# One written order for the first sixteen attention tiles in a fused attention and expert kernel

## The chip, the cores and the metric

The kernel runs on one core of a Trainium2 chip. The metric is the device time of one execution in microseconds (us); less is better. TensorE (PE) does the matmuls and transposes, VectorE (DVE) the elementwise arithmetic, ScalarE (ACT) the transcendental functions and most copies out of the accumulators, GpSimd (POOL) the indirect transfers, and SyncE (SP) issues nearly all plain transfers.

## The reference

Two stages follow one another. The first is a recurrent attention: for each of 4 batches and 8 heads, a 48 by 48 complex state is decayed at every one of 768 steps by a complex factor per row, takes in the outer product of k and v, and is read by q.

```python
mag = np.sqrt(a_re * a_re + a_im * a_im)
scale = np.minimum(mag, 0.999) / (mag + 1e-06)
for t in range(S):
    new_re = ar * S_re - ai * S_im
    new_im = ar * S_im + ai * S_re
    S_re, S_im = (new_re + kv, new_im)
    y[:, :, t] = np.einsum('bhd,bhde->bhe', q[:, :, t], S_re)
```

The second is a mixture of experts on the 3072 rows of 384 that come out: noisy gate logits, the two best of eight experts with softmax weights, and for each expert `relu(x @ w1) @ w2`, with w1 of 384 by 1024.

## The kernel before

Attention is chunked. A tile n is 128 time steps of one batch with all heads; n runs from 0 to 23, four tiles (the four batches) make a group g, and two tiles make a pair m. Inside a chunk the recurrence becomes matmuls; between chunks a state Z per batch is carried.

The change and the prediction name the instructions by an engine letter (A for ScalarE, D for VectorE, P for TensorE), a step and, behind the point, the pair or tile:

- For a pair (`p1`, `p2a`, `p2carry`, `p2s`): A1 is Ln of the real part, A2 its Exp, D1 and D2 the tangent and its square, A3 a Ln, D3 the doubled log magnitude, A4 an Exp, D4 the clipped log decay; A5 is the Arctan, D5 adds the angle carried from the group before, D8 takes absolute values, A7 and A8 are cosine and sine.
- For a tile: P1 sums the angles along time by a triangular matrix, A6 or D6 and D7 take whole turns off (`p2t`); P2 sums the log decays, A9 and A10 are their two Exps, D9 scales q and k by them (`p3`); D10 and D11 multiply q and k by cosine and sine (`p3q`); P3 and P4 transpose q and k, A11 and A12 copy the transposes out (`tr_unit`, line 299); P5a and P5b are the scores, D12a and D12b mask them (`sc_unit`, line 308); P6 is the new part of the state (`st_unit`), D13 adds it to Z (`st_upd`), D15 scales Z (`st_scale`); P7a and P7b make y, A13 copies it out (`y_unit`, line 357); P8 transposes it, A14 copies it (`x_unit`, line 365).
- For a group: G0 is the gate logits (`gate_logits`) and G10 the softmax, the slots and the indirect scatters of rows to the experts' lists (`gate_dispatch`). Their instructions have no names of their own.

All activations go through `phase` (lines 199 and 200), which also orders the loads of the activation table: A1 to A4, A9 and A10 use the table with logarithm and Exp, A5, A7 and A8 the trigonometric one. So there are two table loads in each group, and all A5, A7, A8 of a group stand between them.

Buffers couple the engines: two sets of the three pair tiles `t0`, two `tf`, three `ee`, eight `qk`, six `v`, one PSUM tile `ptr` for the transposes, two `psc` for the scores, two `cum` for P1, P2, P8 and the gates, one `pG` and one `pY`.

Nothing in the program text says which instruction an engine takes next. Each call is entered by `at(step, ...)` at a step number on a time line in which tile n stands at n; the calls are emitted in the order of their steps, and the framework's scheduler then orders every engine's queue by emission order, by priority (`x_unit`, `gate_logits` and `gate_dispatch` have raised ones) and by what its own model of time holds ready. Examples:

```python
at(f - q1 + j * P["d1"], p1, m)
at(n + .5 - P["q"] + i * P["qd"] if n > 1 else f - q3, p3q, n, i)
at(n + P["sc"] + P["sh"] * half, sc_unit, n, half)
at(f - P["lqk"] if g else -14, load_qk, n)
```

The loads stand on SP's one queue. The scatters on POOL wait for the y of a later tile (`PACE`). Behind step 16.5 the expert stage begins to fill in: weights of expert 0 are loaded and split (`load_w1`, lines 501, 502 and 510), its rows are read back and transposed (`x_T`), and its first matmuls (`mm1`, line 564) are put between the last attention tiles. From about 262 us on only expert work is left, with TensorE nearly always at work.

Of the kernel before, what the change touches and what calls it, by code (L numbers as in the profile page):

```python
# [77 lines left out]
def kernel(  # L78
# [21 lines left out]
    NQ = 2  # L100
# [121 lines left out]
    def p1(m):  # L222

        T0[m] = [pf.tile([128, 2, HD], F32, name=f"t0{i}", bufs=2) for i in range(3)]
        ta, tb, th = (flat(x) for x in T0[m])
        ph = 2 * (2 * m // B)
        re, im = flat(RE[m]), flat(IM[m])
        phase(ph, ta, re, AF.Ln)
        i = 2 * m
        phase(ph, tb, ta, AF.Exp, scale=-1.0, accum_out=bad[:, 0, i:i + 1])  # L230
        nc.vector.tensor_mul(th, im, tb)
        nc.vector.tensor_tensor_reduce(tb, th, th, 1.0, 0.0, OP.mult, OP.max, bad[:, 1, i:i + 1])
        phase(ph, tb, tb, AF.Ln, bias=1.0)
        nc.vector.scalar_tensor_tensor(ta, ta, 2.0, tb, op0=OP.mult, op1=OP.add)
        phase(ph, tb, ta, AF.Exp, scale=-0.5, bias=b_eps)
        nc.vector.scalar_tensor_tensor(ta, ta, 2.0 * math.log(0.999), tb, op0=OP.min, op1=OP.subtract)

    def p2a(m):
        th = flat(T0[m][2])
        phase(2 * (2 * m // B) + 1, th, th, AF.Arctan)  # L240

    def p2carry(m):
        if m >= B // 2:
            th = T0[m][2][0:1]
            b = 2 * m % B
            nc.vector.scalar_tensor_tensor(th, car[:, b:b + 2], -2.0 * math.pi, th, op0=OP.mult, op1=OP.add)

    def p2t(n):
        b, g = bt(n)
        pt = psC.tile([128, 512], F32, name="cum")  # L250
        nc.tensor.matmul(pt[:, :HD], tri_t, T0[n // 2][2][:, b % 2, :], start=True, stop=True)
        if n % 2 == 0:
            TF[n // 2] = pf.tile([128, 2, 2, HD], F32, name="tf", bufs=2)
        tf = TF[n // 2][:, :, n % 2, :]
        if g:
            nc.scalar.activation(tf[:, 1, :], pt[:, :HD], AF.Identity, bias=b_rnd)
            nc.vector.scalar_tensor_tensor(tf[:, 0, :], tf[:, 1, :], -RND, pt[:, :HD], op0=OP.add, op1=OP.subtract)
        else:
            nc.vector.tensor_scalar(tf[:, 1, :], pt[:, :HD], RND, -RND, op0=OP.add, op1=OP.add)
            nc.vector.tensor_sub(tf[:, 0, :], tf[:, 1, :], pt[:, :HD])  # L260
        if g + 1 < NG:
            nc.sync.dma_start(car[:, b, :], tf[127:128, 0, :])

    def p2s(m):

        f, a = (flat(TF[m][:, i]) for i in range(2))
        nc.vector.tensor_scalar(a.bitcast(I32), f.bitcast(I32), 0x7FFFFFFF, None, op0=OP.bitwise_and)
        TR[m] = pq.tile([128, 2, 2, HD], F32, name="tr", bufs=4)
        phase(2 * (2 * m // B) + 1, flat(TR[m][:, 0]), a, AF.Sin, scale=-TWO_PI, bias=b_cos)
        phase(2 * (2 * m // B) + 1, flat(TR[m][:, 1]), f, AF.Sin, scale=-TWO_PI)  # L270

    def p3(n):
        b, g = bt(n)
        pt = psC.tile([128, 512], F32, name="cum")
        nc.tensor.matmul(pt[:, :HD], tri_l, T0[n // 2][0][:, b % 2, :], start=True, stop=True)
        EE[n] = pf.tile([128, 2, HD], F32, name="ee", bufs=3)
        ph = 2 * g + 2 if n > 1 else 0
        phase(ph, EE[n][:, 0, :], pt[:, :HD], AF.Exp)
        phase(ph, EE[n][:, 1, :], pt[:, :HD], AF.Exp, scale=-1.0)
        nc.vector.tensor_mul(QK[n], QK[n], EE[n])  # L280
        ec = ecol[g % 3]
        nc.sync.dma_start(es[n:n + 1, :], EE[n][127:128, 0, :])
        for r in range(2):
            nc.sync.dma_start(ec[64 * r:64 * r + D, b, :], es[n].rearrange("(h d) -> d h", h=H))
# [24 lines left out]

    def st_unit(n):  # L310
        b, g = bt(n)
        if g + 1 == NG:
            return
        x = kh[n % NQ]
        for h in range(H):
            for r in range(2):
                nc.tensor.matmul(pG[64 * r:64 * r + D, h, :], x[:, h, r, 0:D], V[n][:, h, :], start=True, stop=True)

    def st_upd(n):
# [5 lines left out]
        if g:  # L325
            nc.vector.tensor_add(Z[b], Z[b], pG)
        else:
            Z[b] = pa.tile([112, H, D], F32, name=f"z{b}")
            nc.vector.tensor_copy(Z[b], pG)

    def st_scale(n):
# [6 lines left out]
        nc.vector.tensor_mul(Z[b], Z[b], FC[g][:, b, :, None].to_broadcast([112, H, D]))  # L338

    def y_unit(n):  # L340
# [292 lines left out]
    pri = {gdis: P["hg"], x_unit: P["hx"], glog: P["hl"]}  # L633
    for g in range(NG):
        f = B * g + .5
        q1, q2, q3 = P.get(f"s{g}", (P["p1"], P["p2"], P["p3"]))
        for j in range(B // 2):
# [3 lines left out]
            at(f - q2, p2a, m)  # L641
            at(f - q2, p2carry, m)
            at(f - q2 + .01, p2s, m)
        for j in range(B):
            n = B * g + j
            at(f - P["lqk"] if g else -14, load_qk, n)
            at(f - q2 + j * P["dt"], p2t, n)
            at(f - q3 + j * P["d3"] if n > 1 else f - q2 - .25, p3, n)
            for i in range(2):
                at(n + .5 - P["q"] + i * P["qd"] if n > 1 else f - q3, p3q, n, i)  # L650
    for n in range(NT):
        at(n + .5 - P["lv"], load_v, n)
        for i in range(2):
            at(n - P["tr"] + P["tk"] * i, tr_unit, n, i)
        for half in range(2):
            at(n + P["sc"] + P["sh"] * half, sc_unit, n, half)
        at(n + P["st"], st_unit, n)
        at(n + P["y"], y_unit, n)
        at(n + P["up"], st_upd, n)
# [295 lines left out]
```

## Time and profile before

| | us |
|---|---|
| median of 3 runs | 716.5 (715.35 to 717.31) |
| the profiled execution's own time | 712.03 |
| its span, first to last instruction | 710.3 |
| TensorE busy in the span | 663.7 (93%) |
| VectorE busy | 411.6 (58%) |
| ScalarE busy | 327.2 (46%) |
| GpSimd busy | 164.4 (23%) |

The profiled execution is 4.5 us shorter than the median of the timed ones, and 1.7 us longer than its span. Busy shares are means over two unlike stages, attention up to about 262 us and experts behind it. TensorE's records overlap, since its matmuls are pipelined and their ends are modelled.

### The profile page before, as it was taken

What the parts mean: (1) busy time and instruction counts of PE and PEld (TensorE: products, weight loads), DVE (VectorE), ACT (ScalarE), POOL (GpSimd) and SP (SyncE); (2) the same over time, 40 slices, a digit from 0 to 9 for tenths busy, and PEclk for the clock granted to TensorE, in tenths of its full rate; (3) what the DMA queues carried; (4) which work ended last, traced back from release to release, by engine and by line L of the source; (5) the groups of instructions that cost most, each with busy time, mean ns of one, the idle gap of its engine ahead of it and who ended that gap; (6) DMA issues with size and microseconds to landing.
All of it is one profiled execution on the core that took longest, in us unless ns stands there. A gap on an engine that the chain in (4) does not pass through costs nothing. (4 is left out here: it accounts for less than half of the span.)

```text
span 710.3 us, 13286 instructions
## 1 busy us (share of the span) xinstructions
PE 663.7 (93%) x5120; PEld 592.7 (83%) x5120; DVE 411.6 (58%) x907; ACT 327.2 (46%) x541; POOL 164.4 (23%) x183
## 2 busy tenths in 40 slices
PE   1579999999999999999999999999999999999995
PEld 0367687878888979898998998998999899899995
DVE  6788899999998757545237325425524624524311
ACT  5679989897955551324115215215313413413300
POOL 2000001323323225112323122222321411412311
PEclk9879999999999999999999999999999999999998
DMA  7477876653466517225228125325415515502201
GB/s 266 118 228 193 278 204 219 211 194 83 142 167 234 198 67 265 93 77 187 64 82 261 32 82 189 116 85 172 133 42 179 172 42 172 173 23 69 65 33 36
DMA packets 63902, 100.24 MB, mean 141 GB/s; under 512 B 26264, under 2 KB 45989, under 8 KB 63824
## 3 DMA queue, kind: packets, MB, share of 16 engines
q1 hardware_dynamic: 54464, 71.68, 32.7%
q0 software_dynamic: 9360, 27.54, 11.1%
q8 instruction: 46, 0.75, 0.4%
q14 instruction: 32, 0.26, 0.1%
HBM read 68.55 MB, written 31.69 MB: 141 GB/s over the span
## 5 line engine op out<-in xcount | busy, mean ns | idle before, releaser
L613 PE MATMUL po<-w2h,h 128*128 128x384 f32 x768 | 204.2, 339 | 2.1 <-DVE ao L624 2.1
L564 PE MATMUL ph<-x,w1h 128*128 128x512 f32 (+2 forms) x720 | 187.3, 349 | 1.3 <-DVE h L570 0.8
L613 PEld LDWEIGHTS po<-w2h,h 128*128 128x128 f32 x768 | 139.4, 188 | 3.7 <-DVE ao L624 3.6
L564 PEld LDWEIGHTS ph<-x,w1h 128*128 128x128 f32 x720 | 125.7, 189 | 18.8 <-DVE h L570 2.1
L613 PE MATMUL po<-w2l,h 128*128 128x384 f32 x384 | 128.6, 335 | 0.0
L564 PE MATMUL ph<-x,w1l 128*128 128x512 f32 (+2 forms) x360 | 124.6, 347 | 0.0
L625 POOL DMA_INDIRECT out_dram<-ao,ox x52 | 50.9, 979 | 268.0 <-DVE ao L624 238.3
L570 DVE SCALAR_TENSOR_TENSOR h<-ph,h 128x512 fp32r<-128x512 f32 (+2 forms) x144 | 70.0, 506 | 68.5 <-ACT h L566 68.4
L566 ACT ACTIVATE h<-ph 128x512 fp32r<-128x512 f32 (+2 forms) x120 | 60.0, 507 | 102.6 <-PE ph L564 85.4
L624 DVE SCALAR_TENSOR_TENSOR ao<-po,gw,ao 128x384 f32<-128x384 f32 (+1 forms) x52 | 31.8, 613 | 125.1 <-PE po L613 124.8
L421 POOL DMA_INDIRECT xs<-xr,sl x48 | 52.8, 1101 | 207.1 <-ACT t L200 104.3
L545 ACT CAST x<-px 128x512 fp32r<-128x512 f32 (+1 forms) x42 | 21.4, 518 | 125.6 <-PE px L540 125.5
L564 PEld LDWEIGHTS ph<-x,w1l 128*128 128x128 f32 x360 | 68.1, 189 | 7.9
L613 PEld LDWEIGHTS po<-w2l,h 128*128 128x128 f32 x384 | 72.3, 188 | 0.1
L589 POOL DMA_INDIRECT ao<-out_dram,ox x49 | 54.4, 1111 | 51.9 <-DMA out_dram<-ao,ox 32.2
L307 PE MATMUL psc<-qT,kT 112*128 112x128 f32 x384 | 52.1, 281 | 0.0
L307 PEld LDWEIGHTS psc<-qT,kT 112*128 112x128 f32 x384 | 48.1, 196 | 2.5 <-issue 1.1
L356 PE MATMUL pY<-am,v 128*48 128x128 f32 x384 | 41.3, 275 | 1.5 <-DVE am L308 1.5
L501 ACT CAST w2h<-raw 128x768 fp32r<-128x768 f32 x32 | 26.4, 836 | 32.5 <-PE po L613 17.3
L502 DVE TENSOR_TENSOR w2l<-raw,w2h 128x768 fp32r<-128x768 f32 x32 | 30.5, 958 | 14.3 <-ACT w2h L501 13.3
L298 PE MATMUL ptr<-ident,qh 128*112 128x128 f32 x192 | 30.2, 289 | 8.6 <-ACT kT L299 7.9
L308 DVE TENSOR_TENSOR am<-psc,mask 128x512 f32<-128x512 f32 x48 | 32.6, 686 | 7.8 <-PE psc L307 7.7
(210 smaller groups left out, 947.9 us busy)
## 6 DMA issues: line engine op xcount, KB each, us to landing
raw<-in_moe_w_dram SPq DMA_DIRECT2D x24, 512.0 KB, 6.7
raw<-in_moe_w_dram SPq DMA_DIRECT2D x32, 384.0 KB, 3.7
qk<-in_qk_dram SPq DMA_DIRECT2D x24, 384.0 KB, 4.1
xgb<-xs SPq DMA_DIRECT2D x8, 800.0 KB
re<-in_a_dram SPq DMA_DIRECT2D x12, 384.0 KB, 3.3
im<-in_a_dram SPq DMA_DIRECT2D x12, 384.0 KB, 7.1
v<-in_v_dram SPq DMA_DIRECT2D x24, 192.0 KB, 2.5
out_dram<-zero SPq DMA_DIRECT2D x12, 384.0 KB, 5.1
```

The lines of the kernel that those rows point to most:

```text
L307: nc.tensor.matmul(p[:, j, :], KT[n][:, h, :], QT[n][:, h, :], start=True, stop=True)
L308: LAST['am'] = nc.vector.tensor_mul(AM[n][:, 4 * half:4 * half + 4, :], p, mask[:, None, :].to_broadcast([128, 4, 128]))
L356: nc.tensor.matmul(o, V[n][:, h, :], AM[n][:, h, :], start=not g, stop=True, skip_group_check=True)
L421: d = nc.gpsimd.indirect_dma_start(out=xs, out_offset=bass.IndirectOffsetOnAxis(ap=sl[:, kk, b:b + 1], axis=0), in_=XR[g][:, lo + b, :], i ...
L502: d = nc.vector.tensor_tensor(lo, raw_t, hi.bitcast(F32), op=OP.subtract)
L564: LAST['m'] = nc.tensor.matmul(p[:, :c], W1[e, kk][i][:, f * 128:(f + 1) * 128], XW[w, kk][:, j, 0:c], start=(m == 0), stop=(m == len(ms) ...
L566: nc.scalar.activation(h[:, 0:c], p[:, :c], AF.Relu)
L570: LAST['h'] = nc.vector.scalar_tensor_tensor(h[:, dst:dst + b - a], p[:, a:b], 0.0, h[:, a:b].bitcast(F32), op0=OP.max, op1=OP.subtract)
L589: nc.gpsimd.indirect_dma_start(out=ao[j][0:w, :], out_offset=None, in_=out, in_offset=bass.IndirectOffsetOnAxis(ap=OX[e][0:w, j:j + 1], ax ...
L613: LAST['po'] = nc.tensor.matmul(p[:, :DM], HT[w, f][i][:, o:o + 128], W2[f // 2][k2][:, f % 2, :], start=(m == 0), stop=(m == len(ms) - 1))
L624: nc.vector.scalar_tensor_tensor(a, p[0:n, :DM], g, a, op0=OP.mult, op1=OP.add)
L625: nc.gpsimd.indirect_dma_start(out=out, out_offset=bass.IndirectOffsetOnAxis(ap=OX[e][0:n, j:j + 1], axis=0), in_=a, in_offset=None, bound ...
```

## The change

The same instructions are issued; none is added, none goes. A string `ORDER` lists 581 keys: 574 named steps (200 of ScalarE, 204 of VectorE, 170 of TensorE) and the places of seven calls for the gates. It holds tiles 0 to 15 whole but for D13.15, A14.15 and D15.12 and later, of tiles 16 to 19 the steps up to D9 and some behind it, and of pairs 10 and 11 the first steps. Three things are done with it. Each call is emitted at the place of its first key, `-16 + .03 * i`. Loads are emitted early (the first two groups' inputs, six `v` tiles and all constants ahead of everything) or right behind the step that frees their buffer. And on each of ScalarE, VectorE and TensorE every key's first instruction is made to follow the last one of the key before it in the list, without a semaphore: it fixes the order in the queue. Instructions of the gates can still fall between. Tiles behind the list keep their steps. Also, `tf` is now allocated by whichever tile of a pair comes first.

```diff
+    ORDER = """
+        A1.0 A2.0 D1.0 D2.0 A3.0 A1.1 D3.0 A2.1 A4.0 D1.1 D4.0 D2.1 P2.0 A3.1 P2.1 A9.0 D3.1 A10.0 D9.0 A4.1
+        A9.1 D4.1 A10.1 A5.0 D9.1 A5.1 P1.0 P1.1 D6.0 D7.0 P1.2 D6.1 D7.1 D8.0 P1.3 A8.0 D6.2 A7.0 D7.2 D6.3
+        P2.2 D10.0 D7.3 P3.0 D11.0 A8.1 P2.3 D8.1 A11.0 D11.1 P6.0 A7.1 D10.1 P4.0 A1.2 D13.0 P6.1 D13.1 A9.2
+        A2.2 A1.3 D1.2 A10.2 D2.2 A2.3 D9.2 A12.0 D1.3 A3.2 P3.1 A9.3 D2.3 P5a.0 A11.1 D3.2 P5b.0 A3.3 D12a.0
+        A4.2 P4.1 D12b.0 A10.3 D3.3 P7a.0 A12.1 P7b.0 D4.2 A4.3 P5a.1 D9.3 A13.0 P5b.1 D12a.1 A5.2 D10.2 P8.0
+        P7a.1 D11.3 P3.2 A14.0 D5.2 A5.3 D12b.1 A11.2 P1.4 D4.3 P7b.1 A6.4 D5.3 P1.5 A13.1 D7.4 A6.5 D10.3 P1.6
+        D7.5 A6.6 D11.2 P1.7 A8.2 D8.2 P6.2 A6.7 D7.6 A7.2 D7.7 P4.2 D13.2 A8.3 P2.4 D8.3 A12.2 P6.3 A7.3 P5a.2
+        D13.3 A9.4 P2.5 D12a.2 P5b.2 A1.4 P7a.2 D12b.2 A10.4 P3.3 A2.4 D9.4 P7b.2 A9.5 D1.4 A11.3 P2.6 D10.4
...
+        A6.11 P5a.6 A7.4 D7.11 D8.5 P6.5 A8.5 D12a.6 A7.5 P2.8 D11.7 P5b.6 P7b.5 D12b.6 A9.8 A10.8 P2.9 D13.5
+        A13.5 D9.8 P8.4 A1.6 P7a.6 A14.4 A2.6 P6.6 A9.9 P7b.6 D10.8 A10.9 G10.0 A13.6 P3.7 D11.8 P8.6 A11.7
...
+        D7.15 P2.12 D13.8 A8.7 D8.7 P7a.9 D12b.9 A7.7 P6.9 P8.8 D11.11 P7b.9 A14.8 A9.12 P4.10 D13.9 A13.9 P6.10
+        A10.12 A12.10 P8.9 P2.13 A14.9 D9.12 G10.1 A1.8 P5a.10 A9.13 P3.11 A2.8 D11.12 P2.14 A10.13 D12a.10
...
+        D11.13 A7.8 P1.19 D13.12 P4.13 D7.18 A6.19 D11.14 P2.16 A12.13 D7.19 P6.13 D15.11 A8.9 D8.9 P5a.13
+        D11.15 A7.9 P3.14 D12a.13 P5b.13 P7a.13 D12b.13 A11.14 P2.17 A9.16 A10.16 P7b.13 A9.17 A1.10 P4.14
+        A10.17 A13.13 D13.13 P2.18 D9.16 A12.14 G10.2 P6.14 A9.18 A2.10 P3.15 D9.17 A10.18 P5a.14 A11.15 D10.17
...
+        D12b.15 A3.11 P8.14 D3.10 P7b.15 A14.14 D3.11 A4.10 P4.16 D9.19 A13.15 P6.15 A4.11 D4.10 G0.3 A12.16
+        D11.17 P8.15 A5.10
+    """.split()
+    def key(name, ins):
+        K.setdefault(name, []).append(ins)
+        return ins
...
-        phase(ph, ta, re, AF.Ln)
+        key(f"A1.{m}", phase(ph, ta, re, AF.Ln))
...
+    PLACE = {k: -16 + .03 * i for i, k in enumerate(ORDER)}
+    def pos(step, *names):
+        ks = [PLACE[k] for k in names if k in PLACE]
+        return min(ks) if ks else step
+    def behind_key(step, name):
+        return PLACE[name] + .01 if name in PLACE else step
...
-            at(f - P["la"] if g else -20, load_a, m)
-            at(f - q1 + j * P["d1"], p1, m)
+            at(-20 + g if early else behind_key(f - P["la"], f"D1.{m - 2}"), load_a, m)
+            at(pos(f - q1 + j * P["d1"], f"A1.{m}"), p1, m)
...
-            at(f - P["lqk"] if g else -14, load_qk, n)
+            at(-19.5 + g if early else behind_key(f - P["lqk"], f"D11.{n - 8}"), load_qk, n)
...
-        at(n + .5 - P["lv"], load_v, n)
+        at(-18.7 + .01 * n if n < 6 else behind_key(n + .5 - P["lv"], f"P7b.{n - 6}"), load_v, n)
...
-    at(-3, consts2)
+    at(-17, consts2)
     for i in range(N // 256):
-        at(P["co"] + .5 + i, clear_out, i)
+        at(behind_key(P["co"] + .5 + i, f"P8.{i + 3}"), clear_out, i)
...
+    for e in "ADP":
+        ks = [k for k in ORDER if k[0] == e]
+        for a, b in zip(ks, ks[1:]):
+            tc.add_manual_dep(K[b][0].ins, K[a][-1].ins.name, after, reason="order at the start")
```

## Rows read from the trace of the kernel before

**Rows 1.** Busy time by stretch between the A5 steps: us, then each engine's.
```profile
core 0: us, PE busy (x) PEld busy (x) DVE busy (x) ACT busy (x) POOL busy (x), PEclk, DMA share, GB/s
5.72:18.54 12.82, 2.90 (x4) 1.18 (x4) 9.24 (x12) 8.15 (x12) 0.10 (x1) 1.00 0.75 287
18.54:44.23 25.69, 16.93 (x164) 12.26 (x164) 21.67 (x33) 18.58 (x25) 0.00 (x0) 0.80 0.64 174
44.23:74.93 30.70, 27.22 (x255) 21.51 (x256) 25.20 (x39) 28.04 (x43) 0.00 (x0) 0.94 0.67 203
74.93:109.18 34.25, 33.13 (x390) 26.33 (x390) 31.54 (x77) 30.14 (x50) 0.00 (x0) 1.00 0.74 231
109.18:144.78 35.60, 35.03 (x465) 29.91 (x461) 34.34 (x81) 31.22 (x50) 9.77 (x8) 1.00 0.71 218
144.78:181.40 36.62, 35.71 (x467) 29.89 (x464) 34.50 (x82) 30.88 (x50) 12.59 (x14) 1.00 0.47 146
```

**Rows 2.** The same view where attention's end and expert work mix.
```profile
220.00:240.00 20.00, 20.00 (x184) 17.47 (x183) 16.53 (x71) 11.20 (x24) 5.03 (x5) 1.00 0.40 133
```

**Rows 3.** VectorE's waits from 58.1 to 181.4 us: total, times, longest.
```profile
DVE qk L280 <- ACT ee L200: 3.3, 3, 2.1
DVE am L308 <- PE psc L307: 2.6, 4, 1.0
DVE tf L257 <- ACT tf L256: 0.8, 3, 0.4
DVE kh L288 <- PE pG L317: 0.5, 1, 0.5
```

**Rows 4.** Timeline of ScalarE: start, us, line, tiles, [idle before <-releaser].
```profile
7.64 0.84 ACT L200 ACTIVATE t<-re 128x768 f32<-128x768 f32 x1 [1.95 <-DMA re<-in_a_dram]
...
17.25 1.28 ACT L199 ACT_TABLE_LOAD   x1
18.54 1.57 ACT L200 ACTIVATE t<-t 128x768 f32<-128x768 f32 x2
...
31.35 1.64 ACT L200 ACTIVATE ee<-cum 128x384 f32<-128x384 f32 x4
...
35.97 1.04 ACT L299 ACTIVATE kT<-ptr 112x1024 f32<-112x1024 f32 x1
...
44.23 1.58 ACT L200 ACTIVATE t<-t 128x768 f32<-128x768 f32 x2
...
57.17 1.64 ACT L200 ACTIVATE ee<-cum 128x384 f32<-128x384 f32 x4
```

**Rows 5.** Timeline of VectorE, same columns.
```profile
6.72 0.96 DVE L232 CUSTOM_DVE_ANT_0 t<-t 128x768 f32<-128x768 f32 x1
...
25.36 0.96 DVE L288 TENSOR_TENSOR qh<-qk,tr 128x768 f32<-128x768 f32 x1
...
58.08 1.83 DVE L280 TENSOR_TENSOR qk<-qk,ee 128x768 f32<-128x768 f32 x2 [2.14 <-ACT ee L200]
...
63.30 1.28 DVE L308 TENSOR_TENSOR am<-psc,mask 128x512 f32<-128x512 f32 x2
...
65.36 0.55 DVE L329 COPY z<-pG 112x384 f32<-112x384 f32 x1
```

**Rows 6.** Timeline of TensorE: P2 of tiles 0 and 1, transposes of q twice.
```profile
13.42 2.90 PE L275 MATMUL cum<-t,tri_l 128*128 128x384 f32 x4 [13.42 <-DVE t L236]
...
37.06 1.96 PE L298 MATMUL ptr<-ident,qh 128*112 128x128 f32 x8 [5.75 <-ACT kT L299]
...
67.66 1.08 PE L298 MATMUL ptr<-ident,qh 128*112 128x128 f32 x8 [0.45 <-ACT kT L299]
```

**Rows 7.** Busy time and granted clock around the first of those transposes.
```profile
34.00:37.00 3.00, 0.00 (x0) 0.00 (x0) 3.00 (x5) 3.00 (x6) 0.00 (x0) 0.50 0.75 128
```

**Rows 8.** Timeline of SP's issues: a constant, and `qk` of group 1.
```profile
26.02 0.43 SPq L676 DMA_DIRECT2D xs<-none  x1
...
37.97 2.45 SPq L213 DMA_DIRECT2D qk<-in_qk_dram  x4
```

More of the change, by code (lines that the diff above doesn't have):

```diff
@@ L227, in p1 @@
         re, im = flat(RE[m]), flat(IM[m])
-        phase(ph, ta, re, AF.Ln)
+        key(f"A1.{m}", phase(ph, ta, re, AF.Ln))
         i = 2 * m
[L230 to L236, printed above, removed]
+        key(f"A2.{m}", phase(ph, tb, ta, AF.Exp, scale=-1.0, accum_out=bad[:, 0, i:i + 1]))
+        key(f"D1.{m}", nc.vector.tensor_mul(th, im, tb))
+        key(f"D2.{m}", nc.vector.tensor_tensor_reduce(tb, th, th, 1.0, 0.0, OP.mult, OP.max, bad[:, 1, i:i + 1]))
+        key(f"A3.{m}", phase(ph, tb, tb, AF.Ln, bias=1.0))
+        key(f"D3.{m}", nc.vector.scalar_tensor_tensor(ta, ta, 2.0, tb, op0=OP.mult, op1=OP.add))
+        key(f"A4.{m}", phase(ph, tb, ta, AF.Exp, scale=-0.5, bias=b_eps))
+        key(f"D4.{m}", nc.vector.scalar_tensor_tensor(ta, ta, 2.0 * math.log(0.999), tb, op0=OP.min, op1=OP.subtract))
     def p2a(m):
         th = flat(T0[m][2])
-        phase(2 * (2 * m // B) + 1, th, th, AF.Arctan)
+        key(f"A5.{m}", phase(2 * (2 * m // B) + 1, th, th, AF.Arctan))
     def p2carry(m):
@@ L245, in p2carry @@
             b = 2 * m % B
-            nc.vector.scalar_tensor_tensor(th, car[:, b:b + 2], -2.0 * math.pi, th, op0=OP.mult, op1=OP.add)
+            key(f"D5.{m}", nc.vector.scalar_tensor_tensor(th, car[:, b:b + 2], -2.0 * math.pi, th, op0=OP.mult, op1=OP.add))
     def p2t(n):
@@ L250, in p2t @@
         pt = psC.tile([128, 512], F32, name="cum")
-        nc.tensor.matmul(pt[:, :HD], tri_t, T0[n // 2][2][:, b % 2, :], start=True, stop=True)
-        if n % 2 == 0:
+        key(f"P1.{n}", nc.tensor.matmul(pt[:, :HD], tri_t, T0[n // 2][2][:, b % 2, :], start=True, stop=True))
+        if n // 2 not in TF:
             TF[n // 2] = pf.tile([128, 2, 2, HD], F32, name="tf", bufs=2)
@@ L274, in p3 @@
         pt = psC.tile([128, 512], F32, name="cum")
-        nc.tensor.matmul(pt[:, :HD], tri_l, T0[n // 2][0][:, b % 2, :], start=True, stop=True)
+        key(f"P2.{n}", nc.tensor.matmul(pt[:, :HD], tri_l, T0[n // 2][0][:, b % 2, :], start=True, stop=True))
         EE[n] = pf.tile([128, 2, HD], F32, name="ee", bufs=3)
         ph = 2 * g + 2 if n > 1 else 0
-        phase(ph, EE[n][:, 0, :], pt[:, :HD], AF.Exp)
-        phase(ph, EE[n][:, 1, :], pt[:, :HD], AF.Exp, scale=-1.0)
-        nc.vector.tensor_mul(QK[n], QK[n], EE[n])
+        key(f"A9.{n}", phase(ph, EE[n][:, 0, :], pt[:, :HD], AF.Exp))
+        key(f"A10.{n}", phase(ph, EE[n][:, 1, :], pt[:, :HD], AF.Exp, scale=-1.0))
+        key(f"D9.{n}", nc.vector.tensor_mul(QK[n], QK[n], EE[n]))
         ec = ecol[g % 3]
@@ L297, in tr_unit @@
         for h in range(H):
-            nc.tensor.transpose(p[:, h, :], x[:, h, :, :].rearrange("p r x -> p (r x)")[:, 0:112], ident)
-        nc.scalar.activation(store[n], p, AF.Copy)
+            key(f"P{3 + i}.{n}", nc.tensor.transpose(p[:, h, :], x[:, h, :, :].rearrange("p r x -> p (r x)")[:, 0:112], ident))
+        key(f"A{11 + i}.{n}", nc.scalar.activation(store[n], p, AF.Copy))
     def sc_unit(n, half):
@@ L306, in sc_unit @@
             h = 4 * half + j
-            nc.tensor.matmul(p[:, j, :], KT[n][:, h, :], QT[n][:, h, :], start=True, stop=True)
+            key(f"P5{'ab'[half]}.{n}", nc.tensor.matmul(p[:, j, :], KT[n][:, h, :], QT[n][:, h, :], start=True, stop=True))
         LAST['am'] = nc.vector.tensor_mul(AM[n][:, 4 * half:4 * half + 4, :], p, mask[:, None, :].to_broadcast([128, 4, 128]))
+        key(f"D12{'ab'[half]}.{n}", LAST['am'])
     def st_unit(n):
@@ L316, in st_unit @@
             for r in range(2):
-                nc.tensor.matmul(pG[64 * r:64 * r + D, h, :], x[:, h, r, 0:D], V[n][:, h, :], start=True, stop=True)
+                key(f"P6.{n}", nc.tensor.matmul(pG[64 * r:64 * r + D, h, :], x[:, h, r, 0:D], V[n][:, h, :], start=True, stop=True))
     def st_upd(n):
@@ L325, in st_upd @@
         if g:
-            nc.vector.tensor_add(Z[b], Z[b], pG)
+            key(f"D13.{n}", nc.vector.tensor_add(Z[b], Z[b], pG))
         else:
             Z[b] = pa.tile([112, H, D], F32, name=f"z{b}")
-            nc.vector.tensor_copy(Z[b], pG)
+            key(f"D13.{n}", nc.vector.tensor_copy(Z[b], pG))
     def st_scale(n):
@@ L353, in y_unit @@
                     if z == 0:
-                        nc.tensor.matmul(o, Z[b][:, h, :], QT[n][:, h, :], start=True, stop=False, skip_group_check=True)
+                        x = nc.tensor.matmul(o, Z[b][:, h, :], QT[n][:, h, :], start=True, stop=False, skip_group_check=True)
                     else:
-                        nc.tensor.matmul(o, V[n][:, h, :], AM[n][:, h, :], start=not g, stop=True, skip_group_check=True)
+                        x = nc.tensor.matmul(o, V[n][:, h, :], AM[n][:, h, :], start=not g, stop=True, skip_group_check=True)
+                    key(f"P7{'ab'[i // 2]}.{n}", x)
         LAST['y'] = YC[n] = nc.scalar.activation(XT[n], pY, AF.Copy)
+        key(f"A13.{n}", YC[n])
     def x_unit(n):
@@ L363, in x_unit @@
         for i in range(H // 2):
-            nc.tensor.transpose(p[:, i * 128:(i + 1) * 128], XT[n][:, i, :], ident)
-        nc.scalar.copy(XR[g][:, b, 0:DM].rearrange("p (h d) -> p h d", h=H),
-                       p.rearrange("p (h x) -> p h x", h=H)[:, :, 0:D])
+            key(f"P8.{n}", nc.tensor.transpose(p[:, i * 128:(i + 1) * 128], XT[n][:, i, :], ident))
+        key(f"A14.{n}", nc.scalar.copy(XR[g][:, b, 0:DM].rearrange("p (h d) -> p h d", h=H),
+                       p.rearrange("p (h x) -> p h x", h=H)[:, :, 0:D]))
     def gate_logits(g, lo, hi):
@@ L651 @@
     for n in range(NT):
-        at(n + .5 - P["lv"], load_v, n)
+        at(-18.7 + .01 * n if n < 6 else behind_key(n + .5 - P["lv"], f"P7b.{n - 6}"), load_v, n)
         for i in range(2):
-            at(n - P["tr"] + P["tk"] * i, tr_unit, n, i)
+            at(pos(n - P["tr"] + P["tk"] * i, f"P{3 + i}.{n}"), tr_unit, n, i)
         for half in range(2):
[L656 to L659, printed above, removed]
@@ L660 @@
-        at(n + .5 + P["xu"], x_unit, n)
-        at(n + .5 + P["ss"], st_scale, n)
+            at(pos(n + P["sc"] + P["sh"] * half, f"P5{'ab'[half]}.{n}"), sc_unit, n, half)
+        at(pos(n + P["st"], f"P6.{n}"), st_unit, n)
+        at(pos(n + P["y"], f"P7a.{n}"), y_unit, n)
+        at(pos(n + P["up"], f"D13.{n}"), st_upd, n)
+        at(pos(n + .5 + P["xu"], f"P8.{n}"), x_unit, n)
+        at(pos(n + .5 + P["ss"], f"D15.{n}"), st_scale, n)
     for g in range(NG):
         for lo, hi in ((0, B),) if g < NG - 2 else ((0, B - 1), (B - 1, B)):
-            at(B * g + hi + .5 + P["gl"], glog, g, lo, hi)
-            at(B * g + hi + .5 + P["gd"], gdis, g, lo, hi)
+            at(pos(B * g + hi + .5 + P["gl"], *[f"G0.{g}"] * (hi - lo == B)), glog, g, lo, hi)
+            at(pos(B * g + hi + .5 + P["gd"], *[f"G10.{g}"] * (hi - lo == B)), gdis, g, lo, hi)
```

57 lines of the change are left out of this document (38 added, 19 removed).

## The prediction

> **What bounds the kernel now.** I read the page first, for the two stages, then busy time by stretch, which tells more than the means of the page. Between the first A5 and the last one in the list VectorE is the fullest engine together with TensorE: in the last two stretches 34.3 of 35.6 and 34.5 of 36.6 us [rows 1]. ScalarE has five us to spare in each. The stretches are cut where A5 of a group starts, so that each holds one round of four tiles. From the first step of VectorE at 5.72 us to 181.40 us its idle time, stretch less busy, is 3.6, 4.0, 5.5, 2.7, 1.3 and 2.1, in all 19.2 us. This is the whole stock from which a better order can take. About two thirds of it lie before 75 us, where there is too little started work to choose from; the steady rounds hold 6.1.
>
> Behind the list TensorE is the bound: 20.00 of 20.00 us between 220 and 240 us [rows 2]. So what the list saves should come out at the end, us for us, as long as weights and gathered rows come earlier too. Nothing in the list touches the expert stage.
>
> Then I read who waits for whom on VectorE in the steady part [rows 3]. 2.6 us are D12 waiting for scores, 0.8 D7 waiting for A6. 3.3 us are D9 waiting for the Exps behind a table load; of these the longest, 2.1, is the one that ends at 58.08 us [rows 5], so 1.2 belong to the three later rounds. That leaves 6.1 - 1.2 = 4.9 for all other causes.
>
> Last, the timelines give start-to-start costs of instructions, by which I walk the list by hand below. A 768 wide step of VectorE repeats after 0.87 us, a half wide one after 0.47 to 0.6, a mask after 0.60. On ScalarE the steps of a pair cost 0.75 to 0.85, A9, A10 0.41, A11 and A12 0.91, A13 0.50, A6 0.50, A14 0.38, a table load 1.28. On TensorE a tile's transposes cost about 0.95 at the full clock, a half of the scores 0.89. The rows give durations; these repeat times are a little shorter, as consecutive records overlap by some 0.08 us (two D9 take 1.83 where one takes 0.95 [rows 5]).
>
> **No instruction is added.** So the cost is only in waits. I cost the first part by a walk, the rest by what it leaves open.
>
> **The first rounds, to D9.4.** Four checkpoints.
>
> First, A5.0. The list puts A3.0 ahead of A1.1, which in the kernel before waited for its input till 7.64 [rows 4]. D2.0 ends at 7.7 [rows 5], so A3.0, A1.1, A2.1, A4.0 follow one another to 11.3, D4.0 ends at 12.3. P2 took 2.90 for two tiles [rows 6], so P2.1 ends at 15.2, and A9.1, A10.1 and the load put A5.0 at 18.05 against 18.54 [rows 4]: 0.5 early.
>
> Second, D10.0. D8.0 now stands before D6.2, so A7.0 is ready by 24.0; but D6.3, which waits for the second `cum` buffer, stands ahead of D10.0, and it starts at 24.55 against 25.36 [rows 5]: 0.8 early. ScalarE gets through A7.1 and the load by 29.95 against 31.35 [rows 4]: 1.4 early.
>
> Third, A5.2. Between that load and A12.0 stand A1.2, A9.2, A2.2, A1.3, A10.2, A2.3, together 4.0: A12.0 at 33.95 against 35.97 [rows 4]. TensorE is idle until then, as it was for 5.75 us before, and its granted clock was 0.50, that is 1.2 GHz, in that time [rows 7]; its next eight transposes took 1.96 where eight at the full clock of 2.4 GHz took 1.08 [rows 6]. I keep the low clock here. So A11.1 waits 0.7 and A12.1 0.9, on top of 8.5 us of ScalarE's work from A12.0 to the end of the next load: A5.2 at 44.2, no earlier than the 44.23 of before [rows 4]. But A12.1 and A13.0 are then done, which used to come behind it.
>
> Fourth, D9.4. From A5.2 ScalarE has 10.7 us of work to the end of the load, with D8 and D7 mostly ahead of their readers since D12b.1, D4.3, D10.3 and D11.2 stand between; with half a us of waits A9.4 starts at 55.4 against 57.17 [rows 4], and D9.4, behind A9.4, A1.4, A10.4, at 57.2 against 58.08 [rows 5]. By then VectorE has done D12a.2, D12b.2 and D13.3, which came at 63.30 and 65.36 before, 1.28 and 0.55 long [rows 5], 1.7 together by repeat times. The lead in work is 0.9 + 1.7 = 2.6 us. The walk's own error I put at 2 either way.
>
> **The steady rounds.** At each change to the Exp table D9 waits for the last A7, the load, and the Exps. What covers it is what stands between D8 and D9 in VectorE's list. Into group 2: A7.5, load, A9.8, A10.8 and 0.2 of handover, 3.1 us, against D12a.6, D11.7, D12b.6, D13.5, 2.5: a wait of 0.6. Into group 3: A7.7, A14.8, load, A9.12, A13.9, A10.12, 4.0, against D12b.9, D11.11, D13.9, 1.9: about 2.0. Into group 4: A7.9, A11.14, load, A9.16, A10.16, 4.05, against D11.15, D12a.13, D12b.13, D13.13, 2.5: 1.5. Together 4.1, where before had 1.2: 2.9 lost. The gates' small steps may fall into these holes (bound: all but nothing of 2.9), but their own Exps wait for the same load, so I count none.
>
> Against it, the other 4.9 us. I walked the whole round from A5.6 to A5.8 and found nothing that is not covered but the load and 0.4 us; a round of three in all leaves 1.2, so 3.7 saved. Bounds: all 4.9 saved, or nothing. In sum 2.9 - 3.7 = -0.8 for the steady rounds, between -4.9 and +2.9.
>
> The Trainium skill, ScalarE: Activation LUTs, "What ACT_TABLE_LOAD costs", puts a change of table at about 2.66 us with the drain behind it, not the load alone. By it each of these three waits would be 1.4 longer, and the list, which covers them less, would lose up to 4.1 and come out 0.7 slower than before. The trace differs: the load at 17.25 lasts 1.28 and the next activation starts at 18.54 [rows 4]; I go by that.
>
> **The moved transfers** I cost at nothing. The eight fills of `xs` (one at 26.02), the `qk` of group 1 (from 37.97) [rows 8] and some of the `v` tiles move forward into the time before 25 us on SP's one queue. The first pair's and second pair's inputs still stand ahead of all of them; the third's are wanted near 30 us. From 5.72 to 18.54 us the transfer engines were busy 0.75 of the time, from there to 44.23 us 0.64 [rows 1], so there is room. If that cover is gone, A1.2 waits: each us there is one of the lead's 2.6. The `car`, `es` and `ecol` transfers queue behind the constants but are read a round later. POOL's scatters hang on A13 of later tiles and move with the list; `out` clearings keep their pace of one a tile.
>
> **The sum.** 2.6 + 0.8 = 3.4 us. On the profiled execution 712.03 becomes 708.6; it stands 4.5 below the median, and I take the same difference from the median: 716.5 - 3.4 = 713.1. What can be told from no change is about 0.3%, 2.15 us.
>
> **The rivals.**
> *The whole stock of waits goes.* If the gates fill the holes at the loads and nothing else waits, the steady rounds give 6.1: 2.6 + 6.1 = 8.7, or 707.8; with the walk's error 706. For it: ScalarE's spare five us a round. Against it: the three chains above are longer than their cover.
>
> *The gain stays in the attention stage.* The list ends some us earlier, but the expert stage's start hangs on its own chain, scatters, read back, weights, or on TensorE's backlog, and the time stays within 2 us of 716.5. For it: TensorE is full from 220 us on, and is 35.0 of 35.6 busy already at 109 us [rows 1], so a lead of VectorE may find TensorE as its wall. Against it: those 35.0 overlap, and TensorE's own work moves forward with the lead.
>
> *The fixed order blocks.* A queue in a fixed order holds everything behind its head. The list waits at places where the free order had other work ready: the holes at the loads. If they cost 4.1 and other waits stay as they are, the steady rounds lose 2.9, and if the early lead is lost to the low clock too, the time is 719.4. It decides from 2.6 us of added waits on. For it: the 5.75 us for which all of TensorE's queue stood behind one transpose [rows 6]. The Trainium skill, PSUM — Partial Sum Buffer, "Engine vs sequencer instructions", says that the queues of ScalarE and VectorE are strictly first in, first out and that matmuls keep program order; that wait agrees with it.
>
> **How the numbers follow.** The forecast, 0.40, own range 710 to 716: 0.30 of it faster, 0.10 the same. The whole stock: 0.20, all faster. The gain stays: 0.20, of it 0.04 faster, 0.14 the same, 0.02 slower. The block: 0.20, of it 0.01 faster, 0.02 the same, 0.17 slower. Together 0.55 faster, 0.26 the same, 0.19 slower. The range runs from the whole stock with the walk's error, 706, to just under the block's price, 719; a tenth lies beyond each end.
>
> **What would show it.** In the changed profile: the first Arctan near 18, the first kT copy near 34, the second group's first Arctan still near 44, D9.4 near 57; VectorE's waits for Exps behind loads about 0.6, 2.0 and 1.5; the last Arctan before 181.4 by three us at the same work done; TensorE full behind it, expert matmuls earlier by as much. Wrong would be: a first round no earlier at D9.4; waits at the loads above 4 us, or none; or an early last Arctan and an unmoved first expert matmul.

## The result, and the profile after

The changed kernel takes 725.25 us (median of 4 runs, 723.2 to 725.78) beside 716.65 us for the kernel before (4 runs): a ratio of 1.0117, with a 95% interval from 1.0093 to 1.0141. It is slower by 8.6 us; 713.1 was forecast, with a range from 706 to 719.

One thing has to be known to read the numbers below. The chips that ran these kernels are not equally quick: on one of them the kernel before takes 711.3 us, on the others 716.0 to 716.7. The trace that the prediction was read from (712.03 us) looks to be of the quick kind: a second profile of the kernel before, on the quick chip, took 712.13 and is the same within 0.2 us at the ends of its attention stage and its span. From the y of tile 16 (its A13) to the last A13 these two and the two other traces of the quick chip take 66.8 to 67.2 us, all others 68.8 to 72.1, whatever the kernel. So each run is given as a ratio to the kernel before on its own chip, and times of one trace are compared with those of another up to that y. Ahead of it two executions of one program still lie up to 2.5 us apart (last section).

The same stretches as in [rows 1], cut again where A5 of a group starts:

```profile
core 0: us, PE busy (x) PEld busy (x) DVE busy (x) ACT busy (x) POOL busy (x), PEclk, DMA share, GB/s
5.72:17.98 12.26, 2.90 (x4) 1.18 (x4) 9.29 (x12) 8.08 (x14) 0.11 (x1) 1.00 1.03 392
17.98:45.45 27.47, 20.90 (x162) 15.51 (x164) 20.57 (x31) 19.70 (x27) 0.00 (x0) 0.88 0.76 230
45.45:77.73 32.28, 30.56 (x336) 23.63 (x335) 29.69 (x47) 30.09 (x46) 0.00 (x0) 1.00 0.56 158
77.73:117.73 40.00, 36.06 (x452) 28.61 (x450) 33.90 (x81) 30.16 (x48) 2.48 (x2) 0.96 0.69 224
117.73:155.23 37.50, 33.61 (x376) 27.70 (x374) 32.22 (x74) 30.42 (x49) 11.21 (x11) 0.95 0.52 157
155.23:194.84 39.61, 38.64 (x498) 30.68 (x497) 36.27 (x85) 32.21 (x52) 14.45 (x12) 1.00 0.43 123
```

The rounds got longer, not shorter: 40.00, 37.50 and 39.61 us where [rows 1] has 34.25, 35.60 and 36.62 (the last of them also holds more of TensorE's work, 38.64 us for 35.71). VectorE's idle time in these three is 6.1, 5.3 and 3.3, 14.7 together, against the 6.1 of before: 8.6 more. TensorE, which was idle for 1.1 and 0.6 in the fourth and fifth stretch of before, is idle for 3.9 in both, and its granted clock is below 1.00 there. So the place is the fourth and fifth stretch, and the engine is TensorE. Who it waits for, from 60 to 190 us:

```profile
PE cum L452 <- DVE ohs L445: 6.8, 2, 3.6
PE pY L397 <- issue: 0.7, 1, 0.7
PE pY L397 <- DVE z L381: 0.4, 1, 0.4
```

Two waits make up 6.8 us, and all others are small. TensorE's timeline around them:

```profile
94.33 1.08 PE L340 MATMUL ptr<-ident,qh 128*112 128x128 f32 x8
98.64 0.18 PE L452 MATMUL cum<-ohs,tri_b 128*128 128x8 bf16 x1 [3.23 <-DVE ohs L445]
98.68 0.81 PE L409 MATMUL cum<-ident,xT 128*128 128x128 f32 x4
...
100.06 1.65 PE L317 MATMUL cum<-t,tri_l 128*128 128x384 f32 x2 [0.24 <-ACT xr L410]
101.50 1.50 PE L340 MATMUL ptr<-ident,kh 128*112 128x128 f32 x8
...
134.13 1.04 PE L340 MATMUL ptr<-ident,qh 128*112 128x128 f32 x8
138.77 0.18 PE L452 MATMUL cum<-ohs,tri_b 128*128 128x8 bf16 x1 [3.60 <-DVE ohs L445]
...
139.87 1.82 PE L349 MATMUL psc<-qT,kT 112*128 112x128 f32 x8
141.48 1.92 PE L340 MATMUL ptr<-ident,kh 128*112 128x128 f32 x8
```

L452 is `tri_b` times `ohs` in `gate_dispatch`; with the products of `ones_b` (L450) it counts the tokens of a group that go to each expert, and so gives each its slot. These count matmuls have no key: the list has only the places of the whole calls, G10.0 and G10.1. In the kernel before they waited 0.22 and 0.29 us:

```profile
105.17 0.17 PE L407 MATMUL cum<-ohs,tri_b 128*128 128x8 bf16 x1 [0.22 <-DVE ohs L400]
...
139.91 0.17 PE L407 MATMUL cum<-ohs,tri_b 128*128 128x8 bf16 x1 [0.29 <-DVE ohs L400]
```

Now they stand right behind P3.7 and P3.11, and everything keyed behind them (P8.6, P2.10, P4.7 and so on) waits until VectorE has made `ohs`. Behind each wait eight transposes take 1.50 and 1.92 us, where eight took 1.08 and 1.04 ahead of it: the clock fell (windows below). On VectorE, ahead of the first:

```profile
95.00 0.95 DVE L273 TENSOR_TENSOR t<-im,t 128x768 f32<-128x768 f32 x1
95.87 0.95 DVE L322 TENSOR_TENSOR qk<-qk,ee 128x768 f32<-128x768 f32 x1
96.74 0.18 DVE L52 TENSOR_TENSOR ga4c<-ga4c,nz 128x32 f32<-128x32 f32 x1
...
98.40 0.19 DVE L445 TENSOR_TENSOR ohs<-ga4oh 128x32 bf16<-128x32 f32 x1
...
102.64 0.96 DVE L322 TENSOR_TENSOR qk<-qk,ee 128x768 f32<-128x768 f32 x1 [1.94 <-ACT ee L241]
```

VectorE isn't idle while TensorE waits. It does D1.6 and D9.9, then the gate's chain of small steps. The loss comes back to it afterwards: D9.10 at 102.64 stands 1.94 us for A9.10, whose P2.10 was held behind the count.

Behind the list nothing is regained. The y of tile 16, whose A13 is no longer in the list, comes 8.8 us later than in the trace of before:

```profile
194.49 0.60 ACT L357 ACTIVATE xT<-pY 128x512 f32<-128x512 f32 x1
```

and in the changed kernel:

```profile
203.26 0.60 ACT L401 ACTIVATE xT<-pY 128x512 f32<-128x512 f32 x1 [0.43 <-PE pY L399]
```

The last A13 comes 12.7 us later (274.22 for 261.54), the first expert down matmul 12.8, and the end of the span 13.1; the 4 us that come in between are the chip's, by the 71.0 and 67.1 us from one A13 to the other.

### The profile page after: what moved, and what is told of

Same layout as the page of the kernel before. It is cut to its first block, busy times and chain, and to the rows that moved or that the text cites. A ratio compares the mean times of both kernels' runs of the same rounds, so it can differ in the third digit from the quotient of the medians.

```text
span 723.4 us, 13268 instructions
## 1 busy us (share of the span) xinstructions
PE 671.9 (93%) x5120; PEld 594.3 (82%) x5120; DVE 412.9 (57%) x907; ACT 328.4 (45%) x541; POOL 173.0 (24%) x183
## 5 line engine op out<-in xcount | busy, mean ns | idle before, releaser
L466 POOL DMA_INDIRECT xs<-xr,sl x48 | 60.0, 1249 | 212.5 <-DMA im<-in_a_dram 95.8
L349 PE MATMUL psc<-qT,kT 112*128 112x128 f32 x384 | 54.4, 287 | 1.4 <-DVE h L615 1.3
L350 DVE TENSOR_TENSOR am<-psc,mask 128x512 f32<-128x512 f32 x48 | 32.9, 685 | 12.8 <-PE psc L349 12.6
L399 PE MATMUL pY<-am,v 128*48 128x128 f32 x384 | 37.9, 274 | 0.2 <-DVE am L350 0.2
L397 PE MATMUL pY<-qT,z 112*48 112x128 f32 x320 | 34.3, 279 | 1.1 <-issue 0.7
```

The costliest lines, as they stand in the source:

```text
L349: key(f"P5{'ab'[half]}.{n}", nc.tensor.matmul(p[:, j, :], KT[n][:, h, :], QT[n][:, h, :], start=True, stop=True))
L397: x = nc.tensor.matmul(o, Z[b][:, h, :], QT[n][:, h, :], start=True, stop=False, skip_group_check=True)
L399: x = nc.tensor.matmul(o, V[n][:, h, :], AM[n][:, h, :], start=not g, stop=True, skip_group_check=True)
L466: d = nc.gpsimd.indirect_dma_start(out=xs, out_offset=bass.IndirectOffsetOnAxis(ap=sl[:, kk, b:b + 1], axis=0), in_=XR[g][:, lo + b, :], i ...
```

## Experiments

Theory 1: the two gates' count matmuls hold TensorE's queue. Theory 2, the rival: the fixed order costs by itself, wherever the gates stand. Theory 3: the early and bunched transfers cost. The first four runs were on one chip.

**The count matmuls later.** `gate_dispatch` is cut in two behind `ohs`; the second half is emitted behind P2.11 or P4.11 and tied to it:

```
+    PIN = {0: "P2.11", 1: "P4.11"}
...
+    for g, k in PIN.items():
+        tc.add_manual_dep(GM[g].ins, K[k][-1].ins.name, after, reason="order at the start")
```

> The changed kernel with one thing moved: the count matmuls of the first and second gate (the products of ohs with tri_b and ones_b) are emitted and queued on TensorE later, behind P2.11 for the first gate and behind P4.11 for the second, so that about 4 us of other TensorE work lies ahead of them while VectorE makes ohs; the order of all keyed steps is kept. Theory 1 (TensorE's queue stands behind the count matmuls of the two gates, 3.23 and 3.60 us in the changed kernel's trace, with a low clock and a late VectorE behind each): both waits fall below 0.5 us and the time goes to 716 to 720. Theory 2 (the order of the steps itself is what costs, wherever the gates stand): the waits move to the next steps, 723 to 727. Theory 3 (the early and bunched transfers cost it): no change, 723 to 727.

Measured: 715.95 us, ratio 0.9995 (0.9981 to 1.0010). The whole loss is gone with two blocks of tiny matmuls moved. The first count now starts at 99.62 and the second at 133.24, both without a wait; 5.1 us of other work lie between P3.7 and the first, and the clock stays up. Windows of this kernel:

```profile
95.00:100.00 5.00, 4.95 (x70) 3.67 (x68) 4.93 (x24) 4.38 (x9) 0.00 (x0) 1.00 0.74 201
100.00:105.00 5.00, 5.00 (x61) 4.27 (x57) 5.00 (x15) 3.95 (x7) 1.29 (x1) 1.00 0.72 173
```

and of the changed kernel in the same places:

```profile
95.00:100.00 5.00, 1.58 (x22) 1.19 (x20) 4.40 (x26) 1.75 (x4) 0.00 (x0) 0.90 0.73 184
100.00:105.00 5.00, 4.94 (x49) 3.72 (x50) 2.85 (x7) 2.18 (x5) 2.48 (x2) 0.76 0.81 294
...
140.00:145.00 5.00, 5.00 (x35) 4.11 (x33) 2.94 (x6) 2.44 (x4) 2.51 (x2) 0.66 0.87 296
```

The third last number is the granted clock. What is lacking to 1.00 is (0.10 + 0.24) x 5 = 1.7 us behind the first wait and 0.34 x 5 = 1.7 behind the second.

**The order taken off**, wholly, and from A5.2 on:

```
-    for e in "ADP":
+    for e in "":
```

and

```
+            if ORDER.index(b) > ORDER.index("A5.2"):
+                break
```

> The changed kernel without the dependencies that fix the order of the keyed steps on the three engines; where each step is emitted, and the early loads and constants, stay as in the changed kernel. Theory 1: the count matmuls of the gates then stand behind other work by themselves (the first behind the q and k transposes of the next tile), 715 to 720. Theory 2: without the order the loss is gone, 714 to 719. Theory 3: the transfers are unchanged, so the loss stays, 723 to 727.

> The changed kernel with the order fixed for the first round only (the keyed steps up to A5.2, about the first 45 us); behind it the steps are emitted in the same places and not tied. Theory 1: the two gate waits lie behind 90 us and their count matmuls are free to stand later, 715 to 720. Theory 2: the order's cost in the first round stays (A5.2 was 1.2 us late in the changed kernel), the rest is gone, 717 to 721. Theory 3: 723 to 727.

Measured: 730.16 (ratio 1.0205, 1.0181 to 1.0228) and 729.21 (1.0188, 1.0167 to 1.0209). All three theories were wrong on these two: without its ties the kernel is slower still. The long waits at the counts are gone, but TensorE now waits 4.7 us in five waits for kT copies. So the order isn't the cost; with the blocks away it is worth 14 us (730.16 - 715.95) against the same places untied. These waits are a third of that; where the rest arises isn't shown.

**The transfers as before.** The first 60 us of SP's queue in the order of the kernel before:

```
...
+    sp = [ES[0], ES[1], LV[0], LV[1], EC[0, 0], ... LQ[4], LQ[5], LQ[6], LQ[7], LV[3], LV[4], LV[5]]
+    for a, b in [*zip(sp, sp[1:]), ... ]:
+        tc.add_manual_dep(b.ins, a.ins.name, after, reason="order at the start")
```

> The changed kernel with the transfers of the first 60 us issued in the order of the kernel before (es and ecol of the first tiles ahead of most of v, the constants and the xs fills between the car transfers, qk of tiles 4 to 7 behind them) and the first zero fills of the output behind es of tile 4; the order of the keyed steps is kept. Theory 1: no change, 723 to 727. Theory 2: no change, 723 to 727. Theory 3 (the moved transfers cost it): 716 to 720.

Measured: 724.51, ratio 1.0106 (1.0085 to 1.0127), the changed kernel's time. Theory 3 falls.

**One gate at a time, and the other way round.** On a second chip, the first gate alone moved, and the kernel before with its first two gates' counts forced early (GM is a count's last matmul, U the matmuls of a tile's step):

```
+    for g, us in enumerate(((("tr", 8, 0), ("sc", 7), ("st", 7), ("y", 7)),
+                            (("y", 10), ("tr", 12, 0), ("sc", 11), ("st", 11)))):
+        for u in us:
+            for x in U[u]:
+                tc.add_manual_dep(x.ins, GM[g].ins.name, after, reason="early")
```

> The changed kernel with the count matmuls of the first gate alone moved behind P2.11; those of the second gate stay where the change put them. Theory 1, each gate's block costs its wait and what follows it, and both together cost 9.3 us: about half comes back, 719.5 to 722. If the first block alone sets what follows: 716 to 718. If the second alone does, since what is lost at the first is caught up before it: 723 to 725.

> The kernel before, with none of the change: only the count matmuls of its first two gates are put early in TensorE's queue, ahead of the q transposes of tile 8 and the scores, state and output matmuls of tile 7 for the first, ahead of the output matmuls of tile 10, the q transposes of tile 12 and the scores and state matmuls of tile 11 for the second. By the trace of before TensorE comes there 2.7 and 2.9 us ahead of ohs. Theory 1: two waits of 2 to 3 us at these matmuls, and 5 to 8 us more in all, 721 to 724. If VectorE and ScalarE catch up behind such a wait, as they would were TensorE not the bound of these rounds: 716 to 718.

Measured: 718.87 (ratio 1.0035, 1.0016 to 1.0055) and 724.23 (1.0105, 1.0089 to 1.0120). By these ratios the first block is worth 1.0117 - 1.0035, some 5.9 us, and the second 2.9; the intervals of the three ratios, 1.0 to 1.7 us each way, leave room for halves. The kernel before, with none of the change, loses 7.5 us by the misplaced counts alone, and its y of tile 16 is as late (201.99 for 194.49):

```profile
104.78 0.17 PE L410 MATMUL cum<-ohs,tri_b 128*128 128x8 bf16 x1 [2.81 <-DVE ohs L403]
...
142.30 0.17 PE L410 MATMUL cum<-ohs,tri_b 128*128 128x8 bf16 x1 [1.83 <-DVE ohs L403]
```

That is 4.6 us of waits, and behind the first of them 1.7 us of clock ((0.02 + 0.32) x 5); behind the second the granted clock stays at 1.00.

**What is left in the mended kernel.** On that chip also two additions to the kernel with both counts moved: the transposes of `lt` later, where TensorE stood 1.07 and 2.26 us, and the transfers as before.

> The kernel with both gates' count matmuls moved (716.0 us), and in addition the transposes of lt moved behind P7a.12 for the third gate and behind P5b.19 for the fifth gate's first part, where TensorE stood 1.07 and 2.26 us before them. If each wait on TensorE goes to the end one for one: 712 to 714. If these waits are refilled at the next step: 715 to 717.

> The kernel with both gates' count matmuls moved (716.0 us), and in addition the transfers of the first 60 us in the order of the kernel before. If the early transfers cost something that the gates' blocks hid: 712 to 715. If they do not: 715 to 717.

Measured: 716.66 (ratio 1.0014, 0.9998 to 1.0030) and 715.70 (0.9987, 0.9978 to 0.9997). The first is a miss: of 3.3 us of waits moved nothing comes back; TensorE stands 1.02 us at the next matmuls for a ScalarE copy and 1.27 at later scores. The second is the best kernel here, by an amount that is under the 0.3% that can be told.

**The start, and VectorE's side.** Three runs fell on the quick chip, so two of them were run again, beside the changed kernel and the best one, on an ordinary chip.

> The kernel before once more, unchanged, for a second profiled execution: the first one took 712.0 us where the median of its runs is 716.5, and the prediction was read from it. If that execution was a favourable one: this one takes 715 to 718 and its attention stage ends 3 to 5 us later than 261.5. If its trace stands for the runs: 711 to 713.

> The changed kernel with TensorE's order untouched; on VectorE the two wide steps that stand among the gate's small ones are tied behind ohs: D1.6 and D9.9 for the first gate, D1.8 and D10.12 for the second, so that ohs is made some 1.9 us earlier each time. Theory 1 (TensorE stands at the count matmuls until VectorE has made ohs): the waits of 3.23 and 3.60 us shrink to 1.3 and 1.7, and of the 9.3 us 4 to 5 come back, 720 to 722. If the place in TensorE's queue costs by something else than the late ohs: 723 to 727.

> The kernel with both gates' count matmuls moved and the earlier transfers in the order of before (715.7 us), and in addition A4.1 issued four times in place of once (the same values written again), which puts 2.8 us more on ScalarE ahead of A5.0. This is about the lead of 2.6 us that the prediction counted from the start to the end. If a lead at the start reaches the end: 718 to 719. If the steps behind it have slack for it: 715 to 716.5.

The edits of the second and third (the third on top of the best kernel):

```
+    for k, g in (("D1.6", 0), ("D9.9", 0), ("D1.8", 1), ("D10.12", 1)):
+        tc.add_manual_dep(K[k][0].ins, OHS[g].ins.name, after, reason="order at the start")
...
-        key(f"A4.{m}", phase(ph, tb, ta, AF.Exp, scale=-0.5, bias=b_eps))
+        for _ in range(4 if m == 1 else 1):
+            key(f"A4.{m}", phase(ph, tb, ta, AF.Exp, scale=-0.5, bias=b_eps))
```

Measured there: 712.13; 715.43 (ratio 1.0062, 1.0038 to 1.0086); 714.90 (1.0043, 1.0027 to 1.0059). The first looks like its second case, but the runs of the kernel before on that chip take 711.3 too: the trace stands for the runs of a quick chip, not for the 716.5. The other expectations in us were for an ordinary chip, and no unpadded kernel stood beside the padded one, so these two were left undecided. Again, with all four on one chip:

> The changed kernel unchanged, on one chip with the three kernels beside it, since the last chip ran the kernel before in 711.3 us and the two chips ahead of it in 716.0 and 716.7, and a ratio found on one chip need not hold on another. As on the first chip: ratio 1.010 to 1.014 to the kernel before. If the loss depends on the chip: outside that.

> Both gates' count matmuls moved and the early transfers in the order of before, as in the earlier run (ratio 0.9987 there), on the chip of the changed kernel. Theory 1: 8 to 10 us below the changed kernel, ratio 0.997 to 1.001.

> VectorE's two wide steps tied behind ohs at each of the two gates, on the chip of the changed kernel. Theory 1: 4 to 5 us below the changed kernel. If TensorE's place costs by something else than the late ohs: no difference to it.

> A4.1 issued four times (2.8 us more on ScalarE ahead of A5.0) in the kernel with the count matmuls moved, on its chip. If a lead at the start reaches the end: 2 to 4 us above that kernel. If there is slack for it: within 1 us of it.

Measured, in this order: 723.47 (ratio 1.0100, 1.0079 to 1.0120), 715.28 (0.9983, 0.9969 to 0.9996), 719.93 (1.0043, 1.0027 to 1.0058), 719.93 (1.0049, 1.0032 to 1.0065). The third gives back a little less than was expected, and the fourth costs more. With TensorE's queue untouched, two wide steps of VectorE put behind `ohs` shorten the waits:

```profile
97.14 0.18 PE L454 MATMUL cum<-ohs,tri_b 128*128 128x8 bf16 x1 [1.62 <-DVE ohs L447]
...
135.78 0.18 PE L454 MATMUL cum<-ohs,tri_b 128*128 128x8 bf16 x1 [1.92 <-DVE ohs L447]
```

6.83 us of waits became 3.54, and 3.5 us came back (723.47 - 719.93; 4.1 by the ratios). So it is the late `ohs`, and the fault can be mended on either engine. The padding put A5.0 2.7 us later (20.84 for 18.16), D9.4 2.5 and the y of tile 16 3.75, and cost 4.65 us by the medians, 2.9 by the two profiled spans (717.4 and 714.5). There is no slack at the start: what is lost there arrives at the end, at least us for us. Why it comes to more is open, and an equal lead was not tried.

## Why the prediction was wrong, step by step

**The step that failed** is the sentence on the gates in the steady rounds: "The gates' small steps may fall into these holes [...] so I count none". It weighed them as fillers of VectorE's idle time and didn't ask which queue their results are read by. Each gate has matmuls near its end that no key holds back, so they reach TensorE's queue ahead of their data, and in a fixed order nothing passes them. By the trace this is 3.23 + 3.60 us of waits and 1.7 + 1.7 of low clock, 10.2 together; taking the blocks away gave back 8.7 by the ratios ((1.0117 - 0.9995) x 716.65) and 8.2 on one chip (723.47 - 715.28), so some of it is caught up.

**TensorE as the wall** was there to be read. [rows 1] shows it busy for 35.03 of 35.60 and 35.71 of 36.62 us, fuller than VectorE, whose idle time the sum was made from. A wait of TensorE has next to no slack to vanish in. The rival "the fixed order blocks" had the sign and the kind; its place, the holes at the table loads, was wrong, and its price of 719.4 too small. That TensorE's matmuls keep program order, as the Trainium skill has it (PSUM — Partial Sum Buffer, "Engine vs sequencer instructions"), was cited beside that rival; the trace agrees, at 98.64: P8.6 and P2.10 had their inputs and stood 3.23 us.

**The loads** were better than forecast. Of waits of 0.6, 2.0 and 1.5 for Exps behind a load, the kernel with the counts moved shows one, 1.48 us at 126.55, where 2.0 was forecast. Against it, the 3.7 us that the other waits were to give did not come. From D9.4 to the y of tile 16, by these two marks alone, the four traces with both counts moved lose 0.7 to 2.1 us on the trace of before, where 0.8 was to be saved (a lead of 0.1 to 1.4 at D9.4, counted as below, and of -0.9 to 0.7 at that y). That is inside the bounds, -4.9 to +2.9; the changed kernel, with 9.2 lost, is outside. On the quick chip, in the padded kernel, VectorE is idle for 8.3 us of that stretch where the kernel before was for 6.2, and among its waits are two of the gates' small steps, for which the same view of before has 0.2 us:

```profile
DVE lz L428 <- PE cum L426: 1.3, 2, 0.9
DVE ga4u L40 <- ACT ga4w L241: 0.9, 1, 0.9
```

So the gates' steps wait here as well, where none was counted; no run took these two waits away.

**The first rounds.** Of the four checkpoints A5.0 and A12.0 hold (17.98 for 18.05, 34.26 for 33.95), D10.0 is half a us late (25.04 for 24.55), and from there it slips:

```profile
34.26 1.02 ACT L341 ACTIVATE kT<-ptr 112x1024 f32<-112x1024 f32 x1
...
45.45 0.84 ACT L241 ACTIVATE t<-t 128x768 f32<-128x768 f32 x1
...
57.69 0.49 ACT L241 ACTIVATE ee<-cum 128x384 f32<-128x384 f32 x1
```

A5.2 is 1.25 late, A9.4 2.3, D9.4 2.1 (59.33 for 57.2). I stretched the transposes for the low clock but not the scores behind them:

```profile
37.08 3.62 PE L349 MATMUL psc<-qT,kT 112*128 112x128 f32 x16
```

where the next 16 took 2.05; D12a.0 and D12b.0 stood 1.51 and 0.51 for them. Where the clock came back sooner, A5.2 was nearly on time: the nine other unpadded traces with the whole order have it between 44.35 and 45.85, and D9.4 between 58.35 and 59.72. The other us came behind A5.2: ScalarE took 12.2 us from there to A9.4 (11.2 of work and 1.0 of waits for P1) where I counted 10.7 and 0.5. So D9.4 came 1.25 later than before (59.33 for 58.08), and the lead in work was 1.7 - 1.25 = 0.45 us in place of 2.6: the term was mis-sized, just beyond its bound of 2 (0.1 to 1.4 in the other traces). That a delay there counts in full, the padded start shows; for a lead no run does.

**The moved transfers** at nothing were right within what can be told (ratios 1.0106 for 1.0117, 0.9987 for 0.9995). **The end** took over us for us what the list did: 8.8 us at the y of tile 16, 8.6 in the medians.

With the blocks away the order gives 0.4 to 1.2 us over the kernel before, where 3.4 were forecast. So the early lead and the saving in the steady rounds were both put too high; which small waits decide that is not shown, since the runs can't tell 2 us of them apart.

## What to carry to other kernels

An order written out for some instructions makes every instruction that isn't in it a possible block: list what is left out, and for each ask which queue it stands in and when its input is ready. Start from the engine that is fullest in that stretch, even if the change is about another. A long chain of tiny steps on one engine should be read by its last result: who stands at the head of which queue waiting for it.

## What the runs showed of the hardware

A wait of TensorE can cost more than its length, since the clock may fall behind it; here that did not go by the length. Behind 3.23 and 3.60 us the loss of clock was 1.7 and 1.7 us; with waits of 1.62 and 1.92 the windows of 5 us there and behind give (0.08 + 0.26) x 5 = 1.7 and 0.33 x 5 = 1.65. But the same program on the quick chip waits 1.93 us at the second count and loses nothing:

```profile
135.00:140.00 5.00, 5.00 (x54) 3.83 (x56) 5.00 (x16) 2.78 (x5) 0.18 (x1) 1.00 0.58 171
```

and on the ordinary one, behind 1.92:

```profile
135.00:140.00 5.00, 4.22 (x31) 3.84 (x32) 4.97 (x21) 1.80 (x4) 0.00 (x0) 0.67 0.57 122
```

Nor does the kernel before with its counts forced early, behind 1.83 us. What decides it isn't shown. The Trainium skill, TensorE: Matmul & The Clock Gate, "Part 1: The HAM clock gate", has the two levels, and calls the ramp's cost less than 1% of a typical kernel's span. The two falls here agree with that (3.4 of 723.4 us), but they are two fifths of the 8.6 that the change lost.

Chips differ by 0.7% with the same granted clock. The padded kernel on the quick and on the ordinary chip (0.987 in both) loads its table at 148.06 and 148.23 us, and ends attention 4.9 us apart. The last copy of `xT` in ScalarE's timeline, on the quick chip:

```profile
264.47 0.60 ACT L404 ACTIVATE xT<-pY 128x512 f32<-128x512 f32 x1 [0.71 <-PE pY L402]
```

and on the ordinary one:

```profile
269.38 0.60 ACT L404 ACTIVATE xT<-pY 128x512 f32<-128x512 f32 x1 [0.56 <-PE pY L402]
```

On the ordinary chip TensorE stands 0.98 and 1.62 us for copies of `lt` that it doesn't stand for on the other. The first of them starts 1.20 us behind the end of that table load, although the logits that it copies had ended at 149.03; on the quick chip it starts at once. What makes it late is open.
